# Rows of thresholds and sums carried through DRAM instead of wide transposes on VectorE, with new ranks for the planner

## The chip, the cores and the metric

The kernel runs on one core of one Trainium2 chip. That core has engines that work side by side, each through its own list of instructions in a fixed order: TensorE (PE, matrix products), VectorE (DVE), ScalarE (ACT), GpSimd (POOL), and SyncE (SP), which here only starts transfers. An engine stops at an instruction whose inputs are not there, and what stands behind it stops too. The metric is the device time of one launch in microseconds (us); the time before is 1337.23 us, the median of three runs (1337.0 to 1337.47).

## The reference

Two blocks. The first is attention with a threshold: 8 batches of 8 heads, 576 positions, head size 64. The second is a feed-forward block with a quick GELU over the 4608 rows that the first one leaves (512 features, 2048 hidden).

```python
scale = 1.0 / np.sqrt(q.shape[-1])
scores = scale * np.matmul(q, k.transpose(0, 1, 3, 2))
thresh = np.max(scores, axis=-1, keepdims=True) - tau
scores = np.where(scores >= thresh, scores, -1000000000.0)
scores = scores - np.max(scores, axis=-1, keepdims=True)
attn = np.exp(scores)
attn = attn / (np.sum(attn, axis=-1, keepdims=True) + 1e-09)
attn_out = np.matmul(attn, v)
...
x = attn_out.transpose(0, 2, 1, 3).reshape(B * S, H * D)
h = x @ w_in
g = h * (1.0 / (1.0 + np.exp(-1.702 * h)))
return g @ w_out
```

## The kernel before

**Tiling.** Two heads make a pair, so there are 32 pairs, numbered n from 0 to 31, four to a batch. Scores are kept transposed: keys lie on partitions, queries on the free axis. Nine key blocks j of 64 keys make five tiles t (four of two blocks, a last of one). The partitions of a tile hold two halves of the queries, each with 64 keys.

**What is done for a pair.** `load_qk` and `load_v` bring the inputs. `prep` (L464) turns q and k in blocks of 32 on VectorE. `scores_run` (L492) multiplies on TensorE in quarters of its array, and `keep` (L496) copies each block from PSUM to SBUF on ScalarE. `in_groups` (L502) takes maxima over groups of 32 keys of one tile and `over_tiles` (L512) over the tiles. `over_halves` (L522) subtracts the gap (from tau) and takes the maximum over the two groups of 32 partitions that hold a query's keys. Now each query's threshold stands once, in a 128 x 18 array. It has to be on all 64 partitions that hold that query's scores, along a row of 576 queries. There are two ways to do that:

- `spread_max` (L539) is one wide transpose on VectorE, 128 x 576, of the array read as if each element stood there 32 times;
- `turn_rows` (L534) copies the array into `flat[0]` and turns it into `flat[1]` (128 x 32); `row_out` (L547) writes it as two rows to DRAM and `row_in` (L555) reads each row back to 64 partitions. These transfers are started by SyncE. `BY_DMA` (L931) names the pairs that go this way: 0, 1, 3, 4, 5, 6, 7.

`sub` (L562, VectorE) then subtracts the threshold from each of the five tiles, `mask` (L568) and `exps` (L572) follow on ScalarE. The sums of the exponentials come from TensorE for the pairs 0 to 4 (`sums_by_pe` and `one_row`), and from VectorE for the others: `in_groups` and `over_tiles` again with addition, `one_group` (L623, four copies and four additions that fold the partition groups and put the sums of a head on that head's rows), and `spread_sums` (L637, a reciprocal and a wide transpose into `rc`). `values` (L591) multiplies by v on TensorE, and `place_x` (L651) multiplies the result by `rc` into `xT`, the input of the feed-forward block.

**Feed-forward.** Rows go in 18 blocks of 256. Blocks 0 and 1 are done by `first_blocks` (L967): 64 tasks of TensorE products (`mm1_0`, `mm2`), which may not start before the pairs 0 to 3 are placed; the products of the first layer also need their pieces of the weights. Blocks 2 to 13 go through `feed_forward` (L997) and the last four through `two_blocks` (L1060), with fewer products by Strassen's scheme (`product`, `read`). In between, `tanh` runs on ScalarE and `gelu` on VectorE; a `gelu` reads the PSUM bank and with that frees it for the next product (two banks, `psM`). Weights arrive as 64-bit numbers in 32 pieces and are turned into 32-bit ones by `cv_ex`, `cv_frac`, `cv_end` on VectorE and `cv_power` on ScalarE.

**What sets the order.** No order is written out by hand. Each step is a task with an engine, a cost, a rank, the tasks that it comes after, and the buffers that it takes and gives back (`task`, L220). `run_in_order` (L233) plays this through on the host while the program is built: whenever an engine is free, it takes the ready task of lowest rank, and emits its instructions. What comes out is a fixed list for each engine. The rank of a task is its pair's number plus a bias by name, from the tables `EARLY` (pairs 0 to 3), `SECOND` (4 to 7), `LATER` (8 to 31) and `CV` (weights), and `W_RANK` spreads the weight pieces. For a transfer through DRAM the planner counts 0.6 us on SyncE and 3.3 until it has landed on the way out, 1.0 and 5.2 on the way back. From pair 7 on, the `values` of pair n - 2 and the `scores_run` of pair n alternate on TensorE without anything between them, since they share buffers.

Of the kernel before, what the change touches and what calls it, by code (L numbers as in the profile page):

```python
# [10 lines left out]
FP32 = mybir.dt.float32  # L11
# [4 lines left out]
ALU = mybir.AluOpType  # L16
# [3 lines left out]
P = 128  # L20
GELU_SCALE = 1.702
EPS = 1e-9
# [8 lines left out]
def kernel(  # L31
# [34 lines left out]
    nc = tc.nc  # L66
# [3 lines left out]
    KT = P // 2  # L70
# [36 lines left out]
        for x in range(2)  # L107
# [5 lines left out]
    flat = [const.tile([P, 32], FP32, name=f"flat{j}") for j in range(2)]  # L113
    gap = const.tile([P, 1], FP32, name="gap")
# [10 lines left out]
              "raw0": 1, "raw1": 1, "qkT0": 1, "qkT1": 1, "v_m0": 1, "v_m1": 1, "w64_0": 1, "w64_1": 1, "row": 1, "rc": 1}  # L125
    for x in ("raw0", "raw1", "qkT0", "qkT1", "mb"):
# [6 lines left out]
        "exps": -13.03,  # L133
        "in_groups": 3.54,
        "keep": 8.7,
        "load_qk": -0.35,
        "load_v": 3.02,
        "mask": -4.3,
        "one_group": -16.49,
        "one_row": 10.29,  # L140
        "over_halves": 4.51,
        "over_tiles": -2.08,
        "place_x": -19.47,
        "prep": -10.76,
        "row_in": 6.33,
        "row_out": 13.15,
        "scores_run": 17.81,
        "spread_max": -2.62,
        "spread_sums": 6.57,
        "sub": 6.26,  # L150
        "sums_by_pe": 0.52,
        "turn_rows": -2.02,
        "values": 6.25,
        "w_sum": 2.08,
        "x_sum": -12.81,
    }
    SECOND = {
        "exps": -9.22,
        "in_groups": 17.42,
        "keep": 18.09,  # L160
        "load_qk": -6.19,
        "load_v": 2.25,
        "mask": -4.66,
        "one_group": 1.4,
        "one_row": -7.39,
        "over_halves": -5.63,
        "over_tiles": -0.54,
        "place_x": -17.43,
        "prep": 1.16,
        "row_in": -11.07,  # L170
        "row_out": -10.78,
        "scores_run": -2.82,
        "spread_max": 8.98,
        "spread_sums": 4.05,
        "sub": 6.07,
        "sums_by_pe": 26.56,
        "turn_rows": -2.56,
        "values": 3.27,
        "w_sum": -0.95,
        "x_sum": 0.01,  # L180
    }
    LATER = {
        "exps": 3.18,
        "in_groups": 6.02,
        "keep": 0.05,
        "load_qk": -5.33,
        "load_v": 3.86,
        "mask": 11.98,
        "one_group": -4.73,
        "one_row": -15.77,  # L190
        "over_halves": 0.98,
        "over_tiles": 0.3,
        "place_x": 4.38,
        "prep": 4.34,
        "row_in": 6.22,
        "row_out": 6.41,
        "scores_run": -12.36,
        "spread_max": -11.89,
        "spread_sums": -3.87,
        "sub": -1.6,  # L200
        "sums_by_pe": -3.04,
        "turn_rows": 14.13,
        "values": -6.55,
        "w_sum": 4.92,
        "x_sum": 4.0,
    }
    CV = {
        "cv_end": -9.13,
        "cv_ex": 4.45,
        "cv_frac": 2.56,  # L210
        "cv_power": -3.6,
        "load_w": -6.63,
# [102 lines left out]
    def seat(tag, x=0):  # L315
        o, size = room[tag][x]
        return arena2[:, o : o + size]
# [204 lines left out]
    def over_halves(n):  # L522
        r = stats[n, ALU.max]
        o = work.tile([P, QB], FP32, name="fold", tag="fold", bufs=1)
        for x in range(4):
            nc.vector.tensor_scalar(  # L526
                out=o[ts(x ^ 1, 32)], in0=r[ts(x, 32)], scalar1=gap[ts(x, 32)], scalar2=None,
                op0=ALU.subtract,
            )
        nc.vector.scalar_tensor_tensor(  # L530
            out=r, in0=r, scalar=gap, in1=o, op0=ALU.subtract, op1=ALU.max
        )

    def turn_rows(n):  # L534

        nc.vector.tensor_copy(out=flat[0][:, 0:QB], in_=stats[n, ALU.max])
        nc.vector.transpose(out=flat[1], in_=flat[0])
# [85 lines left out]
    def one_group(n):  # L623
        s = stats[n, ALU.add]
        o = work.tile([P, QB], FP32, name="fold", tag="fold", bufs=1)
        for x in range(4):
            nc.vector.tensor_copy(out=o[ts(x ^ 1, 32)], in_=s[ts(x, 32)])
        r = work.tile([P, QB], FP32, name="r", tag="r")
        for h in range(2):
            for c in range(2):  # L630
                nc.vector.scalar_tensor_tensor(
                    out=r[ts(h, D), ts(c, QB // 2)], in0=s[ts(c, KT), ts(h, QB // 2)], scalar=EPS,
                    in1=o[ts(c, KT), ts(h, QB // 2)], op0=ALU.add, op1=ALU.add,
                )
        rcs[n] = r

# [264 lines left out]
    nc.gpsimd.memset(flat[0], 0.0)  # L901
    nc.gpsimd.memset(ones, 1.0)
# [28 lines left out]
    BY_DMA = (0, 1, 3, 4, 5, 6, 7)  # L931
# [6 lines left out]
    W_RANK = (16.81, 18.37, 9.14, 15.61, 0.39, 3.55)  # L938
# [211 lines left out]
    for n in range(NP):  # L1150
# [77 lines left out]
        a = task("DVE", 1.05, r, over_halves, n, after=[a, tau_done])  # L1228
        if n in BY_DMA:
            a = task("DVE", 0.4, r, turn_rows, n, after=[a], take=("row",))  # L1230
# [36 lines left out]
        else:  # L1267
# [6 lines left out]
            else:  # L1274
# [5 lines left out]
                a = task("DVE", 1.6, r, one_group, n, after=[a])  # L1280
        exped[n] = ws + su
        summed[n] = task("DVE", 1.05, r, spread_sums, n, after=[a], take=("rc",))
# [38 lines left out]
```

## Time and profile before

| | |
|---|---|
| median of three runs | 1337.23 us |
| time of the profiled execution | 1339.0 us |
| its span, first to last instruction | 1337.1 us |
| mean granted TensorE clock | 0.981 |
| ScalarE busy | 48% of the span |
| VectorE: maxima and sums in groups (L506) | 359.9 us |
| VectorE: thresholds subtracted (L564) | 196.4 us |

In the profile, busy time is given per engine; "PE" is TensorE's products and "PEld" its weight loads, which lie beside them. The 40 slices show busy tenths over the span, each some 33.4 us long. An instruction group is written as line, engine, operation, written and read tile with their shapes, count, busy time, mean of one, and then idle time of the engine just before it with what ended that. `arena` is the large SBUF array in which scores, thresholds and `rc` lie; `part`, `red`, `fold` and `r` are the small arrays of the reductions.

### The profile page before, as it was taken

What the parts mean: (1) busy time and instruction counts of PE and PEld (TensorE: products, weight loads), DVE (VectorE), ACT (ScalarE), POOL (GpSimd) and SP (SyncE); (2) the same over time, 40 slices, a digit from 0 to 9 for tenths busy, and PEclk for the clock granted to TensorE, in tenths of its full rate; (3) what the DMA queues carried; (4) which work ended last, traced back from release to release, by engine and by line L of the source; (5) the groups of instructions that cost most, each with busy time, mean ns of one, the idle gap of its engine ahead of it and who ended that gap; (6) DMA issues with size and microseconds to landing.
All of it is one profiled execution on the core that took longest, in us unless ns stands there. A gap on an engine that the chain in (4) does not pass through costs nothing.

```text
span 1337.1 us, 22553 instructions
## 1 busy us (share of the span) xinstructions
PE 1268.7 (95%) x9128; PEld 983.2 (74%) x9128; DVE 1051.7 (79%) x1720; ACT 646.0 (48%) x830; POOL 246.7 (18%) x290
## 2 busy tenths in 40 slices
PE   5739899899999999999999999999999999999998
PEld 2426774357777777777878777777777778888887
DVE  7899899899999888878788888878787892662642
ACT  4885473866565545555455554454555540210210
POOL 1012111002122120302121202121121216120120
PEclk8869999899999999999999999999999999999999
DMA  8597875545221212111212121211211010000000
GB/s 157 178 240 212 248 222 132 90 93 86 46 42 36 52 37 52 27 44 21 51 36 52 36 52 37 52 37 27 51 29 34 19 34 0 17 1 24 9 0 32
DMA packets 245473, 88.48 MB, mean 66 GB/s; under 512 B 229626, under 2 KB 233722, under 8 KB 245370
## 3 DMA queue, kind: packets, MB, share of 16 engines
q1 hardware_dynamic: 231642, 49.02, 18.4%
q0 software_dynamic: 11360, 37.74, 9.5%
q8 instruction: 71, 1.16, 0.3%
q10 hardware_dynamic: 2368, 0.30, 0.2%
q14 instruction: 32, 0.26, 0.1%
HBM read 73.36 MB, written 9.47 MB: 62 GB/s over the span
## 4 chain that ended last, share of the span: by engine, by line
PE 57%; DVE 26%; ACT 7%; issue 4%; DMA 4%; SPq 2%; DVEq 0%; ACTq 0%
PE ops L865 22%; PE hps L674 10%; PE pv L585 7%; PE ps L483 6%; DVE part L506 6%; DVE arena L564 6%; PE ps L779 4%; PE ps L865 4%; ACT arena L574 3%; PE ops L779 3%; DVE arena L686 2%; ACT arena L570 2%; DVE fold L526 2%; DVE arena L467 2%; ACT arena L500 1%
## 5 line engine op out<-in xcount | busy, mean ns | idle before, releaser
L506 DVE TRANSPOSE_TENSOR_REDUCE part<-arena 128x36 f32<-128x1152 f32 (+1 forms) x295 | 359.9, 1239 | 92.9 <-ACT arena L500 83.5
L674 PE MATMUL hps<-xT,w_in 128*128 128x256 f32 x1536 | 339.7, 381 | 2.7 <-DVE arena L686 2.6
L674 PEld LDWEIGHTS hps<-xT,w_in 128*128 128x128 f32 x1536 | 290.4, 190 | 51.0 <-DVE arena L686 7.0
L500 ACT COPY arena<-ps 128x576 f32<-128x576 f32 x288 | 171.2, 645 | 174.2 <-PE ps L483 174.1
L570 ACT ACTIVATE arena<-arena 128x1152 f32<-128x1152 f32 (+1 forms) x160 | 169.3, 1058 | 153.2 <-DVE arena L564 153.2
L483 PE MATMUL ps<-arena 64*64 64x288 f32 x2304 | 178.7, 424 | 41.1 <-ACT arena L574 16.8
L865 PE MATMUL ops<-w_out,arena 128*128 128x256 f32 x896 | 203.5, 382 | 4.0 <-DVE arena L686 4.0
L564 DVE TENSOR_TENSOR arena<-arena 128x1152 f32<-128x1152 f32 (+1 forms) x158 | 196.4, 1290 | 8.2 <-DMA arena<-row 7.7
L574 ACT ACTIVATE arena<-arena,shift,scl 128x1152 f32<-128x1152 f32 (+1 forms) x160 | 200.3, 1252 | 4.2
L865 PEld LDWEIGHTS ops<-w_out,arena 128*128 128x128 f32 x896 | 169.3, 190 | 32.6 <-DVE arena L686 7.8
L831 POOL TENSOR_TENSOR arena<-arena 128x256 f32<-128x256 f32 x56 | 51.9, 927 | 650.4 <-DVE arena L686 541.2
L483 PEld LDWEIGHTS ps<-arena 64*64 64x64 f32 x2304 | 86.9, 139 | 108.4 <-ACT arena L500 30.9
L585 PE MATMUL pv<-arena 64*64 64x288 f32 x2176 | 160.5, 409 | 0.0
L865 PE MATMUL ops<-arena 128*128 128x256 f32 x672 | 150.8, 381 | 0.0
L865 PEld LDWEIGHTS ops<-arena 128*128 128x128 f32 x672 | 127.5, 190 | 19.2 <-issue 2.2
L683 ACT ACTIVATE th<-hps 128x512 f32<-128x512 f32 x112 | 65.9, 588 | 134.3 <-PE hps L674 107.8
L585 PEld LDWEIGHTS pv<-arena 64*64 64x64 f32 x2176 | 82.6, 134 | 54.2 <-issue 12.5
L887 DVE SCALAR_TENSOR_TENSOR osb<-ops,osb 128x256 f32<-128x256 f32 x98 | 39.3, 413 | 59.1 <-PE ops L865 55.9
L686 DVE SCALAR_TENSOR_TENSOR arena<-th,hps 128x512 f32<-128x512 f32 x96 | 64.0, 667 | 24.0 <-ACT th L683 23.4
L714 PE MATMUL hps<-xT,w_in 128*128 128x256 f32 x256 | 58.6, 390 | 3.6 <-DVE arena L720 3.6
L714 PEld LDWEIGHTS hps<-xT,w_in 128*128 128x128 f32 x256 | 49.2, 195 | 13.1 <-DVE arena L720 4.4
L844 POOL TENSOR_TENSOR arena<-arena 128x512 f32<-128x512 f32 x28 | 35.6, 1270 | 115.1 <-PE ops L865 115.1
(110 smaller groups left out, 1107.3 us busy)
## 6 DMA issues: line engine op xcount, KB each, us to landing
arena<-in_v_dram SPq DMA_DIRECT2D x128, 144.0 KB, 3.3
arena<-in_q_dram SPq DMA_DIRECT2D x128, 72.0 KB, 3.1
out_dram<-osb SPq DMA_DIRECT2D x36, 256.0 KB, 2.0
arena<-in_k_dram SPq DMA_DIRECT2D x124, 72.0 KB, 2.5
w_out<-in_moe_w_in_dram POOLq DMA_DIRECT2D x12, 512.0 KB, 7.7
arena<-in_moe_w_out_dram POOLq DMA_DIRECT2D x12, 512.0 KB, 5.4
w_out<-in_moe_w_in_dram POOLq DMA_DIRECT2D x12, 511.6 KB, 9.3
arena<-in_moe_w_out_dram POOLq DMA_DIRECT2D x12, 511.6 KB, 6.2
```

Source lines behind the costliest of these rows:

```text
L483: nc.tensor.matmul(ps[ts(c, KT), h, 0:SH], lhsT=mats[n, 1][ts(h, D), ts(j, KT)], rhs=mats[n, 0][ts(h, D), ts(c, SH)], start=True, stop=True,)
L500: nc.scalar.copy(out=sT[n, t][:, u], in_=pss.pop((n, j))[:, :, 0:SH])
L506: nc.vector.tensor_reduce(out=stats[n, op][:, t * 2 * QB : min(2 * t + 2, NK) * QB], in_=sT[n, t].rearrange("p u h (g d) -> p (u h g) d", ...
L564: nc.vector.tensor_tensor(out=s, in0=s, in1=mbs[n].unsqueeze(1).to_broadcast(list(s.shape)), op=ALU.subtract)
L570: nc.scalar.activation(out=s, in_=s, func=AF.Prelu, alpha=STEEP)
L574: nc.scalar.activation(out=s, in_=s, func=AF.Exp, scale=scl, bias=shift)
L585: nc.tensor.matmul(o[c][ts(h, D), 0:SH], lhsT=left(j, h)[ts(c, KT)], rhs=sT[n, t][ts(c, KT), u, h, :], start=(j == 0), stop=(j == NK - 1),)
L674: nc.tensor.matmul(hidden[j][:, ts(f, BLK)], lhsT=w_in[:, c, ds((f * HF + j) * P, P)], rhs=xTs[blk][:, c, :], start=(c == 0), stop=(c == N ...
L686: nc.vector.scalar_tensor_tensor(out=g[:, :, j, :], in0=two(ths.pop(j)), scalar=1.0, in1=two(hidden.pop(j)), op0=ALU.add, op1=ALU.mult,)
L714: nc.tensor.matmul(hidden[j][:, ts(i, BLK)], lhsT=w_in[:, c, ts(j, P)], rhs=xTs[i][:, c, :], start=(c == 0), stop=(c == NDC - 1),)
L779: nc.tensor.matmul(places[j, x], lhsT=left[:, c, ts(j, P)], rhs=right[:, c, :], start=(c == 0), stop=(c == 1),)
L865: nc.tensor.matmul(banks[blk][k][:, ts(o, HM)], lhsT=left[:, j, :], rhs=right[:, j, :], start=(j == 0), stop=(j == HF - 1),)
```

## The change

All pairs but 2 now send their thresholds through DRAM, so `spread_max` is left for pair 2 alone. For these pairs `over_halves` subtracts the gap only into the two partition groups that are read (1 and 3), and its combined subtraction and maximum, now on two groups of 32 partitions, writes straight into `flat[0]`; the copy in `turn_rows` is gone. The buffer `row` is taken one step earlier. For the pairs 8 to 31 the sums go the same way: `turn_sums` folds them with four copies and one addition over all partitions, takes the reciprocal into `flat_s[0]` and turns it; `sums_out` writes it to DRAM, and `sums_in` reads it back into `rc`. `one_group` and `spread_sums` are left for the pairs up to 7 (those that used them). All ranks are new; of the tables only some lines are shown.

```diff
--- before.py
+++ after.py
@@ -111,6 +111,7 @@
     neg = const.tile([P, 1], FP32, name="neg")
     scl = const.tile([P, 1], FP32, name="scl")
     flat = [const.tile([P, 32], FP32, name=f"flat{j}") for j in range(2)]
+    flat_s = [const.tile([P, 32], FP32, name=f"flat_s{j}") for j in range(2)]
     gap = const.tile([P, 1], FP32, name="gap")
     stop = const.tile([P, 1], FP32, name="stop")
     shift = const.tile([P, 1], FP32, name="shift")
@@ -122,7 +123,7 @@
     tasks = []
     NXT = 5
     limits = {"psA": 3, "psM": 2, "s_m": 8, "s_t": 2, "io": 2, "hs": 2, "osb": 2, "xT": NXT, "mb": 1,
-              "raw0": 1, "raw1": 1, "qkT0": 1, "qkT1": 1, "v_m0": 1, "v_m1": 1, "w64_0": 1, "w64_1": 1, "row": 1, "rc": 1}
+              "raw0": 1, "raw1": 1, "qkT0": 1, "qkT1": 1, "v_m0": 1, "v_m1": 1, "w64_0": 1, "w64_1": 1, "row": 1, "row_s": 1, "rc": 1}
     for x in ("raw0", "raw1", "qkT0", "qkT1", "mb"):
         limits[x + "_apart"] = 1
     limits["s_m_apart"] = NKT
@@ -130,86 +131,95 @@
 
 
     EARLY = {
...
-        "place_x": -19.47,
...
-        "spread_sums": 6.57,
-        "sub": 6.26,
...
-        "turn_rows": -2.02,
...
+        "place_x": -17.11,
...
+        "spread_sums": 7.14,
+        "sub": 9.27,
...
+        "sums_in": -9.39,
+        "sums_out": 2.13,
+        "turn_rows": -12.55,
+        "turn_sums": -0.41,
...
     }
     SECOND = {
...
-        "place_x": -17.43,
...
-        "spread_sums": 4.05,
-        "sub": 6.07,
...
-        "turn_rows": -2.56,
...
+        "place_x": -20.26,
...
+        "spread_sums": -2.29,
+        "sub": 14.98,
...
+        "sums_in": 7.43,
+        "sums_out": 4.05,
+        "turn_rows": -3.84,
+        "turn_sums": 4.03,
...
     }
     LATER = {
...
-        "place_x": 4.38,
...
-        "spread_sums": -3.87,
-        "sub": -1.6,
...
-        "turn_rows": 14.13,
...
+        "place_x": -0.34,
...
+        "spread_sums": -6.73,
+        "sub": 2.14,
...
+        "sums_in": 3.78,
+        "sums_out": 2.16,
+        "turn_rows": 12.26,
+        "turn_sums": 0.29,
...
     }
     CV = {
...
-        "cv_ex": 4.45,
...
+        "cv_ex": 2.22,
...
     }
 
     LAG = {"PE": 0.26, "DVE": 0.18, "ACT": 0.22, "POOL": 0.18}
@@ -522,18 +532,24 @@
     def over_halves(n):
         r = stats[n, ALU.max]
         o = work.tile([P, QB], FP32, name="fold", tag="fold", bufs=1)
-        for x in range(4):
+        for x in (1, 3) if n in BY_DMA else range(4):
             nc.vector.tensor_scalar(
                 out=o[ts(x ^ 1, 32)], in0=r[ts(x, 32)], scalar1=gap[ts(x, 32)], scalar2=None,
                 op0=ALU.subtract,
             )
+        if n in BY_DMA:
+            for x in (0, 2):
+                nc.vector.scalar_tensor_tensor(
+                    out=flat[0][ts(x, 32), 0:QB], in0=r[ts(x, 32)], scalar=gap[ts(x, 32)],
+                    in1=o[ts(x, 32)], op0=ALU.subtract, op1=ALU.max,
+                )
+            return
         nc.vector.scalar_tensor_tensor(
             out=r, in0=r, scalar=gap, in1=o, op0=ALU.subtract, op1=ALU.max
         )
 
     def turn_rows(n):
 
-        nc.vector.tensor_copy(out=flat[0][:, 0:QB], in_=stats[n, ALU.max])
         nc.vector.transpose(out=flat[1], in_=flat[0])
 
     def spread_max(n):
@@ -633,6 +649,34 @@
                     in1=o[ts(c, KT), ts(h, QB // 2)], op0=ALU.add, op1=ALU.add,
                 )
         rcs[n] = r
+
+    def turn_sums(n):
+
+        s = stats.pop((n, ALU.add))
+        o = work.tile([P, QB], FP32, name="fold", tag="fold", bufs=1)
+        for x in range(4):
+            nc.vector.tensor_copy(out=o[ts(x ^ 1, 32)], in_=s[ts(x, 32)])
+        nc.vector.scalar_tensor_tensor(
+            out=s, in0=s, scalar=EPS, in1=o, op0=ALU.add, op1=ALU.add
+        )
+        nc.vector.reciprocal(out=flat_s[0][:, 0:QB], in_=s)
+        nc.vector.transpose(out=flat_s[1], in_=flat_s[0])
+
+    def sums_out(n):
+        rcs[n] = dram.tile([2, 2, SH], FP32, name="row_s", tag="row_s", bufs=2)
+        for c in range(2):
+            nc.sync.dma_start(
+                out=rcs[n][c].rearrange("h (g i) -> (h g) i", i=32), in_=flat_s[1][ds(c * KT, QB)]
+            )
+
+    def sums_in(n):
+        rc, row = seat("rc"), rcs.pop(n)
+        for h in range(2):
+            nc.sync.dma_start(
+                out=rc[ts(h, D)].rearrange("p (c s) -> p c s", c=2),
+                in_=row[:, h].unsqueeze(0).to_broadcast([D, 2, SH]),
+            )
+        rcs[n] = rc
 
     def spread_sums(n):
 
@@ -899,6 +943,7 @@
 
     nc.gpsimd.memset(rebias, -896.0 * 2.0**23)
     nc.gpsimd.memset(flat[0], 0.0)
+    nc.gpsimd.memset(flat_s[0], 0.0)
     nc.gpsimd.memset(ones, 1.0)
     nc.gpsimd.dma_start(
         out=tau_b, in_=bass.AP(tensor=tau.tensor, offset=tau.offset, ap=[[0, P], [1, 1]])
@@ -928,14 +973,15 @@
 
 
     BY_PE = 5
-    BY_DMA = (0, 1, 3, 4, 5, 6, 7)
+    BY_DMA = (0, 1, *range(3, NP))
+    SUMS_BY_DMA = range(8, NP)
     LEAD = 6
     WHOLE = 6
 
     FFU = 1.727
     T_RANK = FIRST
 
-    W_RANK = (16.81, 18.37, 9.14, 15.61, 0.39, 3.55)
+    W_RANK = (0, 12.87, 12.51, 22.24, 0, 4.97)
     ready_w, w_loads, w64 = [], [], 0
     for i in range(len(pieces)):
         y = 0 if i < NDC else 2 if i < n_in else 4
@@ -1225,9 +1271,12 @@
                 for j in js:
                     copied(n, r, j, a)
         a = task("DVE", 0.35, r, over_tiles, n, ALU.max, after=mx)
-        a = task("DVE", 1.05, r, over_halves, n, after=[a, tau_done])
+        a = task(
+            "DVE", 0.8 if n in BY_DMA else 1.05, r, over_halves, n, after=[a, tau_done],
+            take=("row",) if n in BY_DMA else (),
+        )
         if n in BY_DMA:
-            a = task("DVE", 0.4, r, turn_rows, n, after=[a], take=("row",))
+            a = task("DVE", 0.21, r, turn_rows, n, after=[a])
             a = task("SP", 0.6, r, row_out, n, after=[a], lag=3.3)
             m = task(
                 "SP", 1.0, r, row_in, n, after=[a], take=own(n, "mb"), give=("row",),
@@ -1277,9 +1326,15 @@
                     for t in range(NKT + 1)
                 ]
                 a = task("DVE", 0.35, r, over_tiles, n, ALU.add, after=su + [pv], give=back)
-                a = task("DVE", 1.6, r, one_group, n, after=[a])
+                if n in SUMS_BY_DMA:
+                    a = task("DVE", 1.35, r, turn_sums, n, after=[a], take=("row_s",))
+                    a = task("SP", 0.6, r, sums_out, n, after=[a], lag=3.3)
+                    summed[n] = task("SP", 1.0, r, sums_in, n, after=[a], take=("rc",), give=("row_s",), lag=5.2)
+                else:
+                    a = task("DVE", 1.6, r, one_group, n, after=[a])
         exped[n] = ws + su
-        summed[n] = task("DVE", 1.05, r, spread_sums, n, after=[a], take=("rc",))
+        if n not in SUMS_BY_DMA:
+            summed[n] = task("DVE", 1.05, r, spread_sums, n, after=[a], take=("rc",))
         if pv is not None:
             valued(n, pv)
     for n in (NP - 2, NP - 1):
```

## The prediction

> **What bounds the kernel now.** I read the page's first two parts, then the busy time by stretches of 10 us, then who waited for whom on PE and on DVE, then DVE's groups with shapes kept apart.
>
> ```profile
> PE 1268.7 (95%) x9128; PEld 983.2 (74%) x9128; DVE 1051.7 (79%) x1720; ACT 646.0 (48%) x830; POOL 246.7 (18%) x290
> PE   5739899899999999999999999999999999999998
> DVE  7899899899999888878788888878787892662642
> PEclk8869999899999999999999999999999999999999
> ```
>
> PE is the bound: 95% busy, and its 68.4 us of idle time (1337.1 - 1268.7) lie almost all in the first eight of the 40 slices. DVE is nearly full in the first third only; later it has room. PE fills its time with feed-forward products, and those may not start before pair 3's rows are placed.
>
> ```profile
> 70.00:80.00 10.00, 1.70 (x24) 0.42 (x16) 9.78 (x17) 4.61 (x7) 1.07 (x2) 0.76 1.06 245
> 80.00:90.00 10.00, 1.25 (x12) 0.87 (x16) 7.23 (x9) 9.83 (x10) 4.23 (x8) 0.50 0.60 139
> 150.00:160.00 10.00, 7.06 (x33) 5.91 (x32) 6.54 (x12) 7.53 (x9) 1.07 (x2) 1.00 0.62 183
> 250.00:260.00 10.00, 6.39 (x56) 2.88 (x54) 9.73 (x19) 9.87 (x10) 0.00 (x0) 0.97 0.26 59
> PE ps L483 <- ACT arena L574: 16.8, 1, 16.8
> DVE arena L564 <- DMA arena<-row: 7.7, 4, 3.8
> DVE arena L467 <- DMA arena<-in_k_dram: 3.4, 1, 3.4
> ```
>
> Columns of the stretches: length, then busy us of PE, weight load, DVE, ACT, POOL, then PE's clock, DMA share, GB/s. Summed over such rows PE idles 50.3 us up to 170 us, 4.7 us at 250 to 270, 4.0 from 300 to 420, 5.8 from 420 to 1100 (about 0.3 a pair), and 3.4 at the end. So this is the map: only the start can give much; from 300 us on there are under 10 us to win.
>
> **What the Trainium skill says.** "DMA: Bandwidth & Descriptors", its part on the fixed cost, gives about 2.0 us for a transfer however small, most of it the receipt of the last write, and more where HBM is loaded. A row takes two in series (out, then back), so an estimate from that page is 4 us plus issue. The trace agrees for quiet queues and shows the load: landing of the way back is 3.2 us in the median (2.9 to 8.1); from `turn_rows` to the first `sub` pair 1 needs 14.6 us (30.6 to 45.2, while weights load), pair 3 10.5, pair 6 9.4. "VectorE: DVE Perf Modes", its part on the three transpose paths, says DVE turns separate 32x32 blocks: this is why a wide transpose of a broadcast fills all rows. It costs 778 ns here, and the narrow one 212 ns.
>
> **The change, part by part.** Durations:
>
> ```profile
> L526 DVE TENSOR_SCALAR fold<-red,gap 32x18 f32<-32x18 f32 x128 | 37.0, 289 | 2.5
> L642 DVE STREAM_TRANSPOSE arena<-r 128x576 f32<-128x576 f32 x32 | 24.9, 778 | 1.1
> L627 DVE COPY fold<-red 32x18 f32<-32x18 f32 x108 | 25.8, 239 | 2.5
> L631 DVE SCALAR_TENSOR_TENSOR r<-red,fold 64x9 f32<-64x9 f32 x108 | 22.2, 205 | 1.9
> L541 DVE STREAM_TRANSPOSE arena<-red 128x576 f32<-128x576 f32 x25 | 19.5, 778 | 0.9
> L530 DVE SCALAR_TENSOR_TENSOR red<-red,gap,fold 128x18 f32<-128x18 f32 x32 | 8.6, 270 | 1.1
> L640 DVE RECIPROCAL r<-r 128x18 f32<-128x18 f32 x32 | 7.9, 246 | 0.3
> L537 DVE STREAM_TRANSPOSE flat<-flat 128x32 f32<-128x32 f32 x7 | 1.5, 212 | 0.2
> L536 DVE COPY flat<-red 128x18 f32<-128x18 f32 x7 | 1.2, 170 | 0.2
> ```
>
> *DVE work from pair 8 on.* Before, threshold and sums cost 4 x 0.289 + 0.270 + 0.778 (L541) = 2.20, and 4 x 0.239 + 4 x 0.205 + 0.246 + 0.778 = 2.80, together 5.0 us. After, the fold is two subtractions and two 32-row combined operations (not in the trace; between the 0.205 of L631 and the 0.289 of L526; I take 0.25): 1.08, plus 0.21; and `turn_sums` 4 x 0.239 + 0.270 + 0.246 + 0.212 = 1.68. That is 2.97: 2.0 us less in each of 24 pairs, 49 us. Hardly any of it lies on the path: the pairs come every 36.4 us (pv starts at 552.36 and 698.15, four pairs), all of it PE work, and DVE idles about 6 us of each. I count 0. Pairs 0, 1 and 3 to 7 lose two subtractions and a copy and gain two small operations for one wide: 1.81 to 1.29, 0.5 us each, 3.6 together; these are in the stretch where DVE is full.
>
> *What DVE waits for.* From pair 11 on the changed order has only about 1.1 us of DVE work between `turn_rows` and `sub 0` of a pair, so DVE stands there until the row is back, and `gelu`, `read` and the other four `sub` queue behind it; PE needs the `gelu` to free its bank psM. With quiet queues (DMA share 0.16 to 0.28 after 420 us) the trip is 0.7 issue out + 1 to 2.6 landing + 1.1 issue back + 3.2 = 6 to 7.6 us; I take 7. DVE is busy 33.3 us in a stretch of 40 there on the mean of 420 to 1100, so 30.3 of 36.4; less 2.0 that is 28.3, and with 7 - 1.1 = 5.9 of waiting 34.2 of 36.4: still under. Sums have 8 us of work ahead of `place_x` at pairs 8 and 9 and 14 to 45 up to pair 29, so they land behind cover; pair 31 has 0.6 and makes DVE wait 6 us once, with `gelu 5` of block 13 behind it: 0 to 4 us, taken as 1, since PE runs pair 31's values (4.4 us) there. Cost of the waits: 0 within -4 and +4 (the 9.8 us of small PE stops after 300 us could shrink or grow).
>
> *SP.* From pair 8 on it gains four issues for a row and four for sums, 96 and 96 in all, about 1.8 us per trip, 3.6 a pair beside some 9 (v 2.7, q and k 4.7, half of two stores 1.9): 13 of 36. Its order is fixed: the way back of a row stands ahead of the loads of q and k two pairs on, which have tens of us. 0.
>
> *The ranks: the start.* I lay the two built programs' DVE orders side by side and sum the durations above up to each step. Neighbouring instructions overlap slightly, so a sum is scaled by 0.92 (from pair 1's first `sub` to `place_x 3`: 74.3 us of wall without idle for a sum of 80.9).
> 1. Sum to the end of `place_x 3`: 116.4 before, 109.5 after. Conversion 13, part of 14 and two in_groups of pair 4 move behind it. -6.9 x 0.92 = -6.3 us.
> 2. Before, DVE idles 3.83 us ahead of `sub 1, 0` for row 1. After, conversions 0 to 2 stand in front (5.6 us more by the sum): gone, less up to 1 for weight pieces that are issued at 25.6 to 28.3 us and land 4.9 to 11.4 later. With step 1 that puts `place_x 3` near 113.5 as far as DVE goes.
> 3. The 16.8 us PE stop at 72 to 89 is the wait for pair 2's exponentials, after which 30 us of queued attention work run to 124.25, the first feed-forward product (L714, and `place_x 3` ends at 123.5). After, `sub 2, 0` stands ahead of three in_groups of pair 3: some 3.3 us earlier, so PE does sums and values of pair 2 in that hole. ACT's last exponential of pair 3 stays near 100 us (row 3 lands near 88 again); from there values 3, pair 4 and 5's scores and their copies (17 x 0.65 on ACT plus conversions) need 15 us. So ACT and PE decide here: first product near 116 instead of 124, -8.
> 4. That lead is not kept whole: the next gate is DVE's. Values 8 need pair 8's last sum, 294.0 on the old order, 289.5 on the new: -4.5 x 0.92 = -4.1. Of DVE's 18.4 us idle between 40 and 300 us, the waits that now have work in front are 3.83, 2.19 (row 3), 3.38 (k of pair 6, whose transposition now stands 4.4 us further back) and 1.69 (rows 6 and 7), 11.1; I let 3 come back as new waits for row 3 and for weights: -8.1. Together -12.2 at values 8, against PE's own reach of -8 - 3.6 - 4.7 = -16: DVE decides, -12.
> 5. After that the PE order is the same, product by product, until pair 30, and the switches between tile shapes are 66 in both, so the lead stays; 1 goes to pair 31.
>
> Sum: -11 us. On the profiled execution (1339.0, its span 1337.1 with 1.9 around it) 1328; on the median shown, 1337.23, which lies 1.8 lower, 1326.
>
> **Rivals.**
> *A. The thresholds' trip becomes DVE's bound (slower).* Place: `sub n, 0` of the 21 pairs 11 to 31. It decides from a trip of 36.4 - 28.3 + 1.1 = 9.2 us. Pairs 1 and 3 show 14.6 and 10.5, but at DMA shares of 0.6 to 1.06. At 10.1 it would cost 0.9 x 21 = 19 us, less the 11: 1345. The same sign, with a smaller cost, comes where `gelu` are held back 1 us a pair: +21 - 11, 1347. Against it: the quiet queues. 0.2.
> *B. The start gives nothing.* Rows and weights land later because conversions begin early and loads follow; then only the fold's 3.6 x 0.92 = 3 remain on DVE's path, given back by pair 31 and new stops: 1334 to 1338, say 1336. For it: DMA share near 1 in the first 200 us. 0.17.
> *C. The start gives all of PE's reach,* -16, and DVE's relief takes half of the stops after 300 us, -4: 1317. 0.13.
> The forecast, 1326 (1321 to 1332): 0.5.
>
> **How the numbers follow.** A measurement here tells 0.2% (2.7 us) from no change. Faster: the forecast, C, and a little of B, 0.66. Same: most of B, 0.13. Slower: A and a rest of B, 0.21. The range goes from C to past B into A's near end: 1317 to 1343.
>
> **What would show it.** Right: the first L758 product (L714 before) at 113 to 119 us; pv of pair 8 at 286 to 292 instead of 300.2; the 16.8 us stop under 8; DVE's waits for rows 4 to 7 us each at 21 pairs (some 120 us in all), DVE busy near 1000, PE's stops after 300 us within 6 to 14 us. Wrong: a pair period over 36.6 us between 500 and 1000 (rival A), or the first product after 122 us (rival B).

## The result, and the profile after

The changed kernel takes 1317.87 us (median of four runs, 1316.23 to 1319.17) against 1337.35 for the kernel before beside it: a ratio of 0.9847 (95% interval 0.9832 to 0.9861), so it is faster by 1.5%, well clear of the noise. Its profiled execution took 1317.9, with a span of 1316.2: 20.9 us less than the span of before.

The page's busy times and its slices:

```profile
PE 1260.9 (96%) x9128; PEld 975.6 (74%) x9128; DVE 1006.1 (76%) x1610; ACT 646.6 (49%) x830; POOL 249.0 (19%) x291
PE   5669999999999999999999999999999999999998
DVE  7989999898888887788777877777888863652642
PEclk8879999999999999999999999999999999999999
```

VectorE loses 110 instructions and 45.6 us. TensorE is full from the fourth slice on; before, it took until about the ninth. The same four stretches of 10 us as before (length, then busy us of PE, weight load, DVE, ACT, POOL, PE's clock, DMA share, GB/s):

```profile
70.00:80.00 10.00, 0.76 (x12) 0.21 (x8) 9.80 (x14) 7.05 (x7) 0.00 (x0) 0.69 1.13 316
80.00:90.00 10.00, 8.42 (x92) 7.45 (x96) 6.09 (x14) 5.53 (x7) 0.00 (x0) 0.63 0.71 110
150.00:160.00 10.00, 10.00 (x48) 8.59 (x46) 9.93 (x17) 8.94 (x12) 3.57 (x6) 1.00 0.47 158
250.00:260.00 10.00, 10.00 (x25) 4.47 (x24) 9.80 (x15) 4.97 (x5) 0.00 (x0) 1.00 0.31 80
```

At 80 to 90 us TensorE now works where it stood, and at 150 and 250 its gaps are gone. TensorE's order in time shows the stop at the start and the two marks of the prediction, the first feed-forward product (L758) and the values of pair 8 (`pv`):

```profile
81.58 7.59 PE L601 MATMUL den<-arena,ones 64*64 64x288 f32 x72 [10.82 <-DVE r L632]
...
117.60 1.99 PE L758 MATMUL hps<-xT,w_in 128*128 128x256 f32 x8
...
288.96 1.20 PE L601 MATMUL pv<-arena 64*64 64x288 f32 x16
```

The stop there is now 10.8 us (16.8 before). I use such marks to see where time was won. They are instants of one profiled execution each, us from the start of its span; the pace is the time from pair 14's values to pair 29's, divided by 15:

| | first product | values 8 | values 14 | values 29 | pace per pair | span |
|---|---|---|---|---|---|---|
| before | 124.25 | 300.16 | 516.41 | 1063.01 | 36.44 | 1337.1 |
| after | 117.60 | 288.96 | 501.96 | 1040.36 | 35.89 | 1316.2 |
| won so far | 6.65 | 11.20 | 14.45 | 22.65 | | 20.9 |

So 11.2 us come before pair 8, as forecast. But another 11.4 come between pair 8 and pair 29, where the forecast had nothing, and 1.7 are given back after that. The question for the runs was where those 11.4 come from.

One more row for that, the stretch from 520 to 1000 us of before and of after:

```profile
520.00:1000.00 480.00, 475.46 (x3578) 377.22 (x3569) 394.73 (x611) 248.93 (x315) 92.84 (x96) 1.00 0.20 40
```

```profile
520.00:1000.00 480.00, 479.59 (x3543) 384.77 (x3543) 377.19 (x566) 251.87 (x315) 93.58 (x98) 1.00 0.26 59
```

TensorE idles 4.5 us of 480 before, 0.4 after. The waits of TensorE in the same stretch of before (what stopped, what it waited for: us in total, times, longest) say at what:

```profile
PE ops L865 <- DVE arena L686: 2.8, 6, 0.6
PE hps L674 <- DVE arena L686: 1.7, 5, 0.6
```

L686 is `gelu`. Over 300 to 1100 us all of TensorE's idle time falls from 9.7 to 4.1 us, and its stops for `gelu` from 6.6 to 2.2.

### The profile page after: what moved, and what is told of

Same layout as the page of the kernel before. It is cut to its first block, busy times and chain, and to the rows that moved or that the text cites. A ratio compares the mean times of both kernels' runs of the same rounds, so it can differ in the third digit from the quotient of the medians.

```text
span 1316.2 us, 22807 instructions
## 1 busy us (share of the span) xinstructions
PE 1260.9 (96%) x9128; PEld 975.6 (74%) x9128; DVE 1006.1 (76%) x1610; ACT 646.6 (49%) x830; POOL 249.0 (19%) x291
## 5 line engine op out<-in xcount | busy, mean ns | idle before, releaser
L718 PE MATMUL hps<-xT,w_in 128*128 128x256 f32 x1536 | 337.2, 380 | 0.5 <-DVE arena L730 0.4
L718 PEld LDWEIGHTS hps<-xT,w_in 128*128 128x128 f32 x1536 | 290.7, 190 | 45.9 <-issue 5.7
L580 DVE TENSOR_TENSOR arena<-arena 128x1152 f32<-128x1152 f32 (+1 forms) x158 | 201.1, 1313 | 20.5 <-DMA arena<-row 20.5
L493 PE MATMUL ps<-arena 64*64 64x288 f32 x2304 | 174.7, 420 | 22.9 <-DVE arena L477 15.3
L493 PEld LDWEIGHTS ps<-arena 64*64 64x64 f32 x2304 | 84.0, 137 | 90.8 <-ACT arena L510 30.4
L740 PE MATMUL ops<-w_out,arena 128*128 128x512 f32 x128 | 57.2, 600 | 3.2 <-DVE w_out L465 2.2
L758 PE MATMUL hps<-xT,w_in 128*128 128x256 f32 x256 | 56.4, 381 | 0.0
```

What stands on the lines that cost most here:

```text
L493: nc.tensor.matmul(ps[ts(c, KT), h, 0:SH], lhsT=mats[n, 1][ts(h, D), ts(j, KT)], rhs=mats[n, 0][ts(h, D), ts(c, SH)], start=True, stop=True,)
L580: nc.vector.tensor_tensor(out=s, in0=s, in1=mbs[n].unsqueeze(1).to_broadcast(list(s.shape)), op=ALU.subtract)
L718: nc.tensor.matmul(hidden[j][:, ts(f, BLK)], lhsT=w_in[:, c, ds((f * HF + j) * P, P)], rhs=xTs[blk][:, c, :], start=(c == 0), stop=(c == N ...
```

## The experiments

Two theories were left after the first runs. **T**: the later pairs run faster because VectorE has 2 us less to do in each. **P**: they run faster because the planner now counts a pause for the trip between a pair's thresholds and its `sub`, and puts `gelu` into that pause; it is the order, and neither the transfer nor the lighter VectorE is needed. The first runs also ask whether the ranks alone, or the operations alone, bring the gain. Every ratio is against the kernel before, run beside it on the same chip.

**1. The new ranks with the old operations.** The kernel before with the four tables and `W_RANK` of after.

```diff
-    EARLY, SECOND, LATER, CV, W_RANK  (before)
+    EARLY, SECOND, LATER, CV, W_RANK  (after)
```

> The kernel before with the new ranks and nothing else. Theory T (two parts: the new order of the start gives 11 us up to pair 8, and the lighter VectorE from pair 8 on gives about 9 more by small PE stops that vanish): only the first part comes, 1324 to 1328 us, first feed-forward product near 118 us, values of pair 8 near 289 to 292, and later pairs every 36.5 us. Rival O (all of it is order): about 1318, pairs every 36.0 us. Rival L (all of it is the lighter VectorE): 1335 to 1340.

Measured 1354.49, ratio 1.0123 (1.0108 to 1.0138): slower, outside all three ranges. First product at 127.64, values 8 at 311.49, pace 36.44 as before. The ranks are not good in themselves: with the old costs and tasks they order the start worse than the old ranks do.

**2. The new operations with the old ranks.** The same swap the other way; the tasks that are new keep their new ranks.

> The changed kernel with all its operations and transfers, but the old ranks everywhere (the three new tasks keep their new ranks). It fills the last field of four: old or new operations, old or new ranks. Theory P (ranks and operations are one set: the start comes from ranks that fit these costs, the pace of the later pairs from the planned trip of the thresholds whatever the ranks): first product near 124 or later, pairs every 35.9 to 36.0 us from pair 14 on, 1327 to 1342 us. If the transfers give their gain on their own: 1318 to 1322. If the pace comes from the new ranks: pairs every 36.4 us.

Measured 1334.13, 0.9971 (0.9944 to 0.9999), just faster. The start is as before (124.14; values 8 at 303.03), but the pace is 35.88. So the start's gain needs the new ranks, while the pace of the later pairs does not.

**3 and 4. Only the thresholds, only the sums** (all with after's ranks).

```diff
-    SUMS_BY_DMA = range(8, NP)
+    SUMS_BY_DMA = ()                      # 3
-    BY_DMA = (0, 1, *range(3, NP))
+    BY_DMA = (0, 1, *range(3, 8))         # 4
```

> The changed kernel, sums spread by VectorE as before for all pairs, so only the thresholds go through DRAM; the planner makes its own order. Theory T: 1.1 us a pair of VectorE's work comes back, 1322 to 1328 us. Theory P: the thresholds' transfer is the one that lets gelu through, pairs every 35.9 to 36.0 us from pair 14 on, and the stretch before decides: 1319 to 1328.

> The changed kernel, thresholds of the pairs from 8 on spread by VectorE as before, so only the sums go through DRAM; the planner makes its own order. Theory T: 0.9 us a pair comes back, 1322 to 1328 us. Theory P: pairs every 36.4 us from pair 14 on as in the kernel before, 1328 to 1336.

Thresholds only: 1324.2, 0.9894 (0.987 to 0.9917), pace 35.90, values 8 at 288.15. Sums only: 1332.22, 0.9953 (0.9936 to 0.9971), first product 117.62, values 8 at 287.01, pace 36.28. The first time lies in the ranges of both theories; it is the two paces that speak for P. So the pace goes with the thresholds' trip, and the start with neither trip of the later pairs. The thresholds-only kernel loses its 6 us between pair 8 and pair 14 (221.8 us there, 213.0 in after). The sums-only kernel loses more there (222.8) than by its pace.

**5. VectorE's load given back, order kept.** The last reduction of each kind is repeated, which adds about the 2 us a pair that the change had taken away; the planner is not told.

```diff
+        for _ in range((2 if op == ALU.max else 3) if n >= 8 else 0):
+            nc.vector.tensor_reduce(out=r, in_=stats[n, op]..., axis=AXL.X, op=op)
```

> The changed kernel, its order kept, with the reduction over the tiles repeated on VectorE from pair 8 on (twice more for the maxima, three times more for the sums, 5 x 0.43 = 2.2 us a pair, writing the same values), which gives back what the transfers took off VectorE. Theory T: most of the later gain goes, 1324 to 1328 us, values of pair 8 unchanged near 289, pairs every 36.4 to 36.5 us. Rival O: 1318 to 1319, since VectorE still idles and the order is unchanged.

Measured 1331.27, 0.995 (0.9934 to 0.9966): 13 us of the gain gone, more than either theory gave, which looks like T. But the place is not T's: pair 8 to 14 take 224.6 us (213.0), while the pace afterwards is 36.03, only 0.14 us above after's. VectorE's waits for rows rise from 20.5 to 42.3 us. So the load costs much only where the pairs are dense. Run 8 has such a load there without the trip and takes 213.4 us, so load and trip together are the likely cause; no run shows them apart.

**6 and 7. Which ranks.** Old `EARLY`, `SECOND`, `CV` and `W_RANK` in the first, old `LATER` in the second.

> The changed kernel with the old ranks for pairs 0 to 7 and the weights (EARLY, SECOND, CV, W_RANK), new ones from pair 8 on. Theory T: the first part of the gain goes, 1326 to 1331 us, first product near 124, values of pair 8 near 299. Rival L: 1318 to 1321. A third way: the stops at the start come back but the later slack of TensorE cannot take anything up, so the loss at pair 8 is the loss at the end, to within 2 us.

> The changed kernel with the old ranks from pair 8 on only (LATER). TensorE's own order from pair 9 on hardly depends on them. Theory T: 1317 to 1322 us, pairs every 36.0 to 36.2 us. Rival O: 1326 to 1328, pairs every 36.5 us.

Old start: 1333.07 (13 runs, 1328.82 to 1337.91), 0.9964 (0.9951 to 0.9977), first product 124.12, values 8 at 302.43, pace 35.88. Old `LATER`: 1324.96, 0.9902 (0.9885 to 0.9918), first product 118.08, pace 35.88 too; it loses 6 us around pair 8 in one stop of TensorE, seen in its waits from 290 to 340 us:

```profile
PE hps L718 <- DVE arena L730: 6.2, 1, 6.2
```

So `LATER` matters where it takes over from `SECOND`, not for the pace.

**8. After's order, before's operations for the pairs from 8 on.** Every task keeps its place; `turn_rows` does the wide transpose, `turn_sums` is `one_group`, `place_x` begins with `spread_sums`, and the four transfer steps are empty.

```diff
     def turn_rows(n):
+        if n >= 8:
+            spread_max(n)
+            return
...
     def row_out(n):
+        if n >= 8:
+            return
```

> The changed kernel's order of tasks kept on every engine, but from pair 8 on with the operations of before: the wide transpose of the thresholds where turn_rows stood, the fold of the sums where turn_sums stood, the reciprocal and the wide transpose of the sums ahead of place_x; no transfers of rows from pair 8 on. Theory T (the lighter VectorE gives the later part, in the stretch of pairs 8 to 13 where VectorE is full): 1325 to 1331 us, values of pair 8 near 290, lead lost by pair 14. Theory P (the order is what counts, and the planner found it because a transfer leaves VectorE free for the gelu of the feed-forward in between): 1317 to 1321 us, pairs every 35.9 us.

In this kernel pair 8's thresholds are written over pair 7's before pair 7 has used them, so four of the five subtractions of pair 7 take other thresholds; the instructions and their number are as described. Measured 1319.33, 0.9861 (0.9842 to 0.988): within 1.5 us of after, with no transfer of rows from pair 8 on and with VectorE as busy as before (1047.4 us; 399.05 of the 480 us from 520 to 1000). Pace 35.96. T is refuted for the pace: the load is back, and the gain stays.

**9. A longer trip.** The row goes through a second place in DRAM before it is read back; VectorE has nothing more to do.

```diff
+        if n >= 8:
+            again = dram.tile([2, S], FP32, name="again", tag="again", bufs=2)
+            nc.sync.dma_start(out=again, in_=row)
+            row = again
```

> The changed kernel, its order kept, with a copy from DRAM to DRAM put between the way out and the way back of the thresholds from pair 8 on, some 2 to 4 us more for each trip. The profile of the changed kernel shows VectorE waiting for rows 20.5 us in all, so most rows land before VectorE comes to them. If that slack is real: 1318 to 1323 us. If the prediction's margin holds (bound by VectorE from a trip of 9.2 us on, and a trip of 7): 1330 to 1360.

Measured 1347.38, 1.0067 (1.0049 to 1.0085): 29 us slower than after, and slower than before. Pace 36.72. VectorE's order in time around one trip, in after and then in this kernel (start, length, the wait ahead of the instruction in brackets):

```profile
662.74 0.21 DVE L553 STREAM_TRANSPOSE flat<-flat 128x32 f32<-128x32 f32 x1
662.88 0.69 DVE L730 SCALAR_TENSOR_TENSOR arena<-th,hps 128x512 f32<-128x512 f32 x1
666.26 0.69 DVE L730 SCALAR_TENSOR_TENSOR arena<-th,hps 128x512 f32<-128x512 f32 x1 [2.69 <-ACT th L727]
668.63 1.82 DVE L580 TENSOR_TENSOR arena<-arena 128x1152 f32<-128x1152 f32 x1 [1.68 <-DMA arena<-row]
```

```profile
681.55 0.21 DVE L553 STREAM_TRANSPOSE flat<-flat 128x32 f32<-128x32 f32 x1
681.91 0.69 DVE L734 SCALAR_TENSOR_TENSOR arena<-th,hps 128x512 f32<-128x512 f32 x1 [0.15 <-ACT th L731]
685.29 0.69 DVE L734 SCALAR_TENSOR_TENSOR arena<-th,hps 128x512 f32<-128x512 f32 x1 [2.69 <-ACT th L731]
690.03 1.36 DVE L584 TENSOR_TENSOR arena<-arena 128x1152 f32<-128x1152 f32 x1 [4.05 <-DMA arena<-again]
```

From the end of the narrow transpose to the `sub`, after needs 5.0 to 5.7 us where VectorE waited for the row; here it is 7.0 to 9.1 (14.8 once, at pair 8). Two `gelu` fit into after's trip; here the next one, due some 3.4 us after the second, has to stand behind the late `sub`. TensorE is busy 472.20 of the 480 us. The hop adds some 2.3 us (medians after 300 us: 7.6 here, 5.3 in after). That lies near the 2.0 us that the Trainium skill gives for a transfer, however small ("DMA: Bandwidth & Descriptors", its part on the fixed cost); the page's figure is for transfers started by GpSimd, and these are started by SyncE.

**10. All the old operations in after's order.** As 8, but with the old folds in the pairs 0 to 7 too, the wide transpose moved to the first `sub`, and more buffers for `red` and `r`, so that every pair has its own thresholds.

> The changed kernel's order of tasks kept on every engine, with all operations of before: full folds and the copy for every pair, from pair 8 on the wide transpose of the thresholds ahead of the first subtraction, the old fold of the sums, and the reciprocal and wide transpose ahead of place_x; no transfers of rows from pair 8 on. VectorE's work is that of the kernel before. Theory P (the order makes the gain, the planner finds it because a transfer leaves VectorE free for gelu): 1319 to 1323 us, values of pair 8 near 291, pairs every 35.9 to 36.0 us. Theory T (the lighter VectorE makes the later part): 1326 to 1332.

Measured 1324.11, 0.9896 (0.9882 to 0.9911), values 8 at 288.59, pace 35.99: between the two ranges in time, as P said in the pace. This is the kernel before in another order, instruction for instruction on the four computing engines but for one memset: 13.8 of after's 19.5 us come from the order alone (each against the kernel before beside it, here 1337.92 - 1324.11). The operations bring the other 5.7. Of these, 4.6 lie between this run and 8, which differ in the old folds in the dense start and in the place of the wide transpose. At values 8 this run is still 0.7 us ahead of 8, so the old folds have cost nothing up to there; it falls behind by 3.3 us between pair 8 and 14. The two were not parted.

**11. Sums through DRAM, thresholds by the wide transpose, order kept.** No thresholds' trip to wait for, the full folds again, and the light sums: if the trip costs after more than the 0.9 us of work that comes back, this beats it.

```diff
     def sub(n, t):
+        if n >= 8 and t == 0:
+            spread_max(n)
```

> The changed kernel's order kept and its sums through DRAM, but from pair 8 on the thresholds by the wide transpose ahead of the first subtraction, with full folds: no trip for VectorE to wait for, 0.9 us more work a pair. Theory P: at least as fast as the changed kernel, 1314 to 1318 us. If the transfers of thresholds themselves save time: 1320 to 1328.

Measured 1319.95, 0.9864 (0.9848 to 0.988), pace 35.92: no better than after, and a miss for P's 1314 to 1318. So the trip, at 5.0 to 5.7 us, costs no more than those 0.9 us a pair of VectorE's work; that it costs nothing is not shown. None of the kernels tried beats after.

**12. The pause alone.** The kernel before, with its own ranks and all its operations; only the planner is told of the trip's costs, by two tasks on SyncE that issue nothing.

```diff
+            if n >= 8:
+                a = task("SP", 0.6, r, pause, n, after=[a], lag=3.3)
+                a = task("SP", 1.0, r, pause, n, after=[a], lag=5.2)
```

> The kernel before with its old ranks and all its operations; only the planner is told that from pair 8 on a threshold takes 10.1 us from its fold to its wide transpose, by two empty tasks with the costs of the two transfers. Nothing waits on the chip. Theory P: the start stays (first product near 124, values of pair 8 near 300), the pairs then come every 35.9 to 36.1 us instead of 36.4: 1325 to 1331 us. Theory T, and any in which the transfers or the new ranks are needed: 1335 to 1345.

Measured 1329.24, 0.9933 (0.9918 to 0.9948), 8.7 us less than the 1337.92 beside it. The start is as before (124.31), the pace is 35.86. Values 8 are no mark here (316.60): the planner put 80 feed-forward products ahead of them. From 400 to 1070 us, though, TensorE's list is the same, product for product by line and tile, before, in after and here, so its own order does not make the pace. The stretch from 520 to 1000 reads

```profile
520.00:1000.00 480.00, 480.00 (x3594) 383.81 (x3591) 400.08 (x639) 248.72 (x316) 97.55 (x95) 1.00 0.20 41
```

TensorE has no idle time left beside a VectorE that does all its old work. That is P, by itself: a new order and nothing else. How it acts is seen in VectorE's order around one pair, before and then here:

```profile
679.08 0.78 DVE L541 STREAM_TRANSPOSE arena<-red 128x576 f32<-128x576 f32 x1
679.78 0.65 DVE L686 SCALAR_TENSOR_TENSOR arena<-th,hps 128x512 f32<-128x512 f32 x1
680.36 3.88 DVE L564 TENSOR_TENSOR arena<-arena 128x1152 f32<-128x1152 f32 x3
...
687.23 1.36 DVE L506 TRANSPOSE_TENSOR_REDUCE part<-arena 128x36 f32<-128x1152 f32 x1
688.52 0.64 DVE L686 SCALAR_TENSOR_TENSOR arena<-th,hps 128x512 f32<-128x512 f32 x1
```

```profile
675.84 0.68 DVE L689 SCALAR_TENSOR_TENSOR arena<-th,hps 128x512 f32<-128x512 f32 x1
679.05 0.69 DVE L689 SCALAR_TENSOR_TENSOR arena<-th,hps 128x512 f32<-128x512 f32 x1 [2.54 <-ACT th L686]
679.66 0.77 DVE L544 STREAM_TRANSPOSE arena<-red 128x576 f32<-128x576 f32 x1
682.51 0.69 DVE L689 SCALAR_TENSOR_TENSOR arena<-th,hps 128x512 f32<-128x512 f32 x1 [2.08 <-ACT th L686]
683.12 3.89 DVE L567 TENSOR_TENSOR arena<-arena 128x1152 f32<-128x1152 f32 x3
```

Before, the wide transpose and the `sub` follow the fold at once, and VectorE does not idle; a `gelu` gets its turn between long operations. The `tanh` of the last one shown had ended near 687.6, but the `gelu` starts at 688.52, behind a reduction of 1.36 us, and TensorE, which needs its bank, stops 0.61 us. With the planned pause two more `gelu` stand ahead of the block of `sub`, and VectorE waits for their `tanh` (2.54 and 2.08 us): it idles where nobody needs it, and each of them runs at the moment that it can.

VectorE is only half of it. ScalarE's order has changed too, and in the example above it cost more:

```profile
685.76 1.35 ACT L574 ACTIVATE arena<-arena,shift,scl 128x1152 f32<-128x1152 f32 x1
687.01 0.58 ACT L683 ACTIVATE th<-hps 128x512 f32<-128x512 f32 x1
689.22 1.13 PE L865 MATMUL ops<-w_out,arena 128*128 128x256 f32 x4 [0.61 <-DVE arena L686]
```

The last line is TensorE's stop. The products for that `tanh` (L683) ended at 684.98, so it stood 2.0 us behind the `mask` and `exps` of the tiles already subtracted, and the `gelu` then 0.9 behind VectorE's reduction. Over all 63 such `gelu` between values 14 and values 29 (mean us from the end of the products to the `tanh`, and from its end to the `gelu`):

| | products to `tanh` | `tanh` to `gelu` | pace |
|---|---|---|---|
| before | 0.56 | 0.77 | 36.44 |
| run 4 | 0.56 | 0.67 | 36.28 |
| run 10 | 0.32 | 0.54 | 35.99 |
| run 8 | 0.22 | 0.55 | 35.96 |
| after | 0.23 | 0.39 | 35.89 |
| run 12 | 0.18 | 0.34 | 35.86 |

Ahead of these 63 `tanh`, ScalarE was busy with `mask` and `exps` for 33.7 us before and 10.0 here. So the order frees TensorE's banks earlier by way of both engines; no run changes one of the two alone.

## Why the prediction was right or wrong

Predicted were 1326 us (1321 to 1332), 11 less; measured are 1317.87, 19.5 less. The 11 came where they were forecast. Step 5, which held that nothing more comes after pair 8, failed.

**Steps 1 to 3, the start: right, within 2 us.** It put `place_x 3` near 113.5 for VectorE and the first product near 116; they came at 115.4 and 117.60, inside the given 113 to 119. Runs 2 and 6, with the old ranks, stay at 124.1, and all kernels with the new ranks and a start like after's lie at 116.5 to 119.1. That the new order gives the start is thus shown. It takes the ranks together with the new costs and tasks (run 1, with the ranks alone, is at 127.64), but not the shorter folds (run 10 has the old ones and is at 116.52). Which of the moves does it (conversions ahead of `sub 1, 0`, or `sub 2, 0` ahead of three in_groups) was not parted. Two signs missed: the stop of 16.8 us was to be under 8 and is 10.8, and TensorE's stops after 300 us were to be 6 to 14 us and are 4.1.

**Step 4, values 8 twelve us earlier: right.** 288.96, 11.2 us earlier, inside 286 to 292. VectorE's last reduction for pair 8's sums ends at 287.47 where it ended at 299.11: 11.6 us earlier, 12.2 predicted. That VectorE decides there is not shown: TensorE does not stop ahead of values 8 in either profile. Of its 11.2 us, 7.9 are idle time, and 3.3 are shorter busy time for the same 2080 products (241.54 us after, 244.82 before, at mean granted clocks of 0.94 and 0.91), a term that the sum did not have.

**The sizes of VectorE's operations: right.** Thresholds cost 2 x 0.308 + 2 x 0.280 + 0.210 = 1.39 us where 1.29 was taken, sums 4 x 0.233 + 0.198 + 0.266 + 0.211 = 1.61 where 1.68 was. Together 3.00, predicted 2.97. That hardly any of this is on the later path ("I count 0") holds too: run 8 does the old operations in the same order at 35.96 a pair against 35.89, which is 1.5 us in 21 pairs.

**Step 5, "the lead stays", with "cost of the waits: 0 within -4 and +4": this failed.** The lead did not stay, it doubled: 11.4 us more from pair 8 to 29, of which 8.2 at the steady pace (15 x 0.55) and 3.2 between pair 8 and 14. The prediction compared TensorE's order and found it the same product by product. It saw the planned pause in VectorE's order and treated it only as a place for waits. It left out what the planner put into it: `gelu` ahead of the block of `sub` rather than behind it, and with the later `sub` fewer `mask` and `exps` in front of `tanh`. That the order does it, run 12 shows by itself: pace 35.86 and 8.7 us less time; that it is these places in the order is read from the traces. Every kernel whose planner counts the thresholds' trip runs at 35.9 to 36.0, whether or not anything is carried (8, 10, 12), but for run 9 with its real delay; before, run 1 and run 4 are slower.

The step's bound was off too: it took the 9.8 us of shown stops after 300 us as all there was, and half of them as the most (rival C). Idle time fell by 5.7 us, while the steady pace alone won 8.2. Between values 14 and values 29, for the same products, TensorE idles 5.14 us before and 0.41 after: 0.31 of the 0.55 us a pair. The other 0.23 lie within what the view counts as busy (541.46 and 537.99 us), 2.9 of these 3.5 us in the two groups that stop for `gelu`, here before and then after:

```profile
L674 PE MATMUL hps<-xT,w_in 128*128 128x256 f32 x993 | 219.8, 381 | 1.8 <-DVE arena L686 1.7
L865 PE MATMUL ops<-w_out,arena 128*128 128x256 f32 x496 | 113.0, 382 | 3.4 <-DVE arena L686 3.4
```

```profile
L718 PE MATMUL hps<-xT,w_in 128*128 128x256 f32 x993 | 218.0, 380 | 0.1
L909 PE MATMUL ops<-w_out,arena 128*128 128x256 f32 x496 | 111.9, 380 | 0.3 <-DVE arena L730 0.3
```

So bounding a gain by the idle time that a profile shows was too tight by nearly half.

**VectorE's waits for rows: wrong in number, and it did not matter.** Predicted 4 to 7 us at 21 pairs, some 120 in all:

```profile
DVE arena L580 <- DMA arena<-row: 20.5, 13, 3.7
```

The trip is 5.0 to 5.7 us where 7 was taken, and the 1.1 us of work counted before `sub 0` left out the `gelu` and their own waits for `tanh`, which fill most of it.

**Rival A, the trip as a bound: a real mechanism, and nearer than said.** It was to decide from a trip of 9.2 us. Run 9 loses already at 7.0 to 9.1: 0.83 us a pair. The arithmetic of 9.2 summed VectorE's time in a pair; what decides, as read from the order around one trip, is when the next `gelu` is due, which is its weaker form ("`gelu` are held back"). Rival B is refuted by the first product and by values 8. Rival C's time was the right one, for another reason: TensorE's whole reach at the start (16 us) was not won, and the later gain is over twice the 4 us that it gave.

**The end.** 1 us was set for pair 31; from values 29 to the last instruction it takes 275.8 us instead of 274.1, with one stop of 1.4 us of TensorE at pair 31.

Two things stay open: how the gain of the pace divides between the `gelu` on VectorE and the `tanh` on ScalarE, and how much of the 3.2 us between pair 8 and 14 is load and how much order. For the second, run 8 keeps the time from pair 8 to 14 (213.4 us) and run 10 does not (216.7), though both do the old operations there; run 11, with the wide transpose where run 10 has it but the light sums, takes 212.4.

## What to carry to other kernels

A short operation that frees the bottleneck's buffer should stand ahead of a long block on its engine, even if the engine then idles. When a change alters what a planner believes, compare the order of exactly these operations, on every engine that they pass, and not only the bottleneck's own list. To part the two, run the new order with the old operations and the old operations with only the new planned cost (here 13.8 and 8.7 of 19.5 us came without any of the change's transfers). Ranks that fit one set of costs and tasks are no asset by themselves: here they cost 1.2% on the old operations.

## What the runs showed of the hardware

VectorE's small operations hardly get cheaper with fewer partitions. Least, median and greatest ns of one, in the kernel before and then in after:

```profile
L530 DVE SCALAR_TENSOR_TENSOR red<-red,gap,fold x32: 236/238/1264, 19.6 to 1077.8; 128x18 f32<-128x18 f32 x32
L536 DVE COPY flat<-red x7: 135/177/178, 19.9 to 232.0; 128x18 f32<-128x18 f32 x7
L627 DVE COPY fold<-red x108: 164/170/1212, 208.5 to 1095.0; 32x18 f32<-32x18 f32 x108
```

```profile
L542 DVE SCALAR_TENSOR_TENSOR flat<-red,gap,fold x62: 225/228/1240, 18.7 to 1053.3; 32x18 f32<-32x18 f32 x62
L659 DVE SCALAR_TENSOR_TENSOR red<-red,fold x24: 178/178/650, 288.7 to 1079.4; 128x18 f32<-128x18 f32 x24
```

In the median the combined operation takes 238 ns on 128 partitions and 228 on 32, a copy 177 and 170. The same form of instruction with a constant in place of the array `gap` (and a sum in place of the maximum) takes 178. So the two halves in `over_halves` cost 0.46 us where one whole operation cost 0.24; what the fold gains is the two subtractions and the copy that it drops.

The means are higher (280 ns for L542, 270 for L530) because a few of these instructions are very long. In six such groups (L526, L627, L631 before; L536, L542, L658 after) 74 instructions took over 300 ns, and for all 74 GpSimd was busy during more than half of that time; of the 495 others that holds for 27. GpSimd's spans in a profile are rough, and what its work does to them no run here shows.

And a row of 576 numbers goes out to DRAM and back onto 64 partitions in 5.0 to 5.7 us, from VectorE's last instruction to its next, while the queues are quiet (DMA share 0.26); in the first 240 us, while weights load, it took 5.9 to 10.7.
